# One slot of a software pipeline in another order: two-bank score tiles, the V products in one visit, a transpose over four quadrants

## The chip, the cores and the metric

The kernel runs on one core of one Trainium2 chip, as one launch. The metric is the device time of that launch in microseconds (us). A core has TensorE (PE, matrix products into PSUM), VectorE (DVE), ScalarE (ACT), GpSimd (POOL) and SyncE (SP); each works through its own queue in order, and they meet at semaphores. PSUM, the accumulator memory, has eight banks of 2 KiB per partition, and in this kernel all eight are in use, so that who holds which bank is part of the schedule.

## The reference

Attention with one added to the softmax's denominator, then a soft mixture of experts with slots, on the attention's output:

```
q, k, v: (8, 12, 448, 64)              # batch, heads, tokens, head size
scores = q @ k.T / 8
m = max(scores, -1);  e = exp(scores - m)
attn = e / (sum(e, -1) + exp(-m) + 1e-9)
x = (attn @ v), heads side by side      # (3584, 768)
logits = x @ phi                        # 32 slots
d = softmax(logits, over tokens);  slot_input = d.T @ x       # 8 experts of 4 slots
slot_out[e] = relu(slot_input[e] @ w1[e]) @ w2[e]             # 768 -> 1024 -> 768
c = softmax(logits, over slots);  out = c @ slot_out
```

## The kernel before, in words

The 96 heads are worked in 48 **pairs** n. A pair has its two heads on partitions 0 to 63 and 64 to 127; 448 tokens are three chunks of 128 (i = 0, 1, 2) and one of 64 (i = 3). For each pair these steps run, each written as a Python function that issues its instructions in order on several engines:

- `T(n)`: 28 transposes of 64x64 on PE (L256) into one PSUM bank of `psB`, then one copy of 128x896 to SBUF, on ACT (L263) or, for 4 pairs of 6 after the first nine, on DVE (L265).
- `A(n, i)`: the scores with queries on partitions, into a bank of `psA` (L285; L304 for i = 3, both heads in one bank), and their row maximum on DVE (L287, L307). `As` takes the next such step from the list `runs`, which is some three to four pairs ahead of the rest. A bank of `psA` is held from the product until the maximum has read it, and the pool has three, given out in turn.
- `W1`, `W2`, `W3`: once for three pairs, the maxima are negated on POOL, turned on PE and copied on ACT.
- `Bk(n, i)`: the scores with keys on partitions, both heads, into two banks of `psB`, minus the maximum by a second product (L367 and L370, or L396 and L399), and an exponential for each bank on ACT (L372, L402). With `mix` the two products of an `A` step are woven in between: `a0` first, `a1` last.
- `AV(n, i, qs)`: products of the exponentials with V (L436), 24 for the full chunks and 8 for the half one in every pair, into the one bank of `psV`.
- `N1`: copy of that bank to SBUF on ACT (L449). `N2`: sum and reciprocal on DVE (L464, L465), then the scaling on POOL (L469 to L480).
- `PX`: four products that turn the result (L501) into a bank of `psB`, and a copy on ACT (L507).

`P(b)` is the slot logits and their softmax for a batch of six pairs; its pieces are put into the slots by the table `post`. All of it is in an order written by hand (no scheduler moves anything). A string `ramp` orders the first three pairs. Then a loop over slots s runs, in two halves y = 0 and y = 1 for each slot: `Bk` i = 0 and 1 with two `A` steps, `AV` of the pair before (12 full products and the 8 half ones), `N1`; then `Bk` i = 2 with an `A` step, `Bk` i = 3 with the `A` step for i = 3, `T(s + 6)`, the first 12 `AV` products of pair s, `PX`, `N2`. POOL also issues the loads of q, k, v and the expert weights (L114, L176, L180, L181). After the loop the expert products and the output run (L853 and after).

The PSUM pools before are `psA` 3 banks, `psB` 4 and `psV` 1.

## Time and profile before

Three runs took 298.0, 298.18 and 299.7 us (median 298.18). The profiled execution has a span of 299.0 us from its first to its last instruction; no other time is recorded for that execution.

| stretch of the span, us | what runs | PE busy | DVE busy | ACT busy | POOL busy |
|---|---|---|---|---|---|
| 0 to 32 | ramp | 26.7 | 27.0 | 21.3 | 22.8 |
| 32 to 235 | slots with `A` steps | 198.8 | 190.7 | 193.6 | 164.6 |
| 235 to 250 | last slots, no `A` steps left | 14.7 | 8.3 | 13.6 | 6.4 |
| 250 to 299 | experts and output | 31.3 | 23.8 | 21.3 | 2.2 |

The table is added up from a view that gives each engine's busy time in stretches of the span. "Busy" of PE is modelled: matmuls are pipelined, and each is counted with its latency, so that 98% busy doesn't say that PE had no time left. DVE and ACT instructions overlap by some 0.1 us with the next one, so their cost in a row of instructions is the distance from start to start, not the duration of one.

### The profile page before, as it was taken

How to read it: one execution, taken by the hardware profiler on the slowest of the kernel's cores; microseconds unless marked ns; L12 is line 12 of the kernel's file. 1: busy time of each engine (PE TensorE's matmuls, PEld its weight loads, DVE VectorE, ACT ScalarE, POOL GpSimd, SP SyncE). 2: the span in 40 equal slices, each digit the busy share in tenths (PEclk: the TensorE clock that was granted, in tenths of full speed). 3: DMA queues.
4: the chain of work that ended last, by engine and by line, in shares of the span. 5: the costliest groups of instructions: out<-in, count | busy, mean ns of one | idle time of the engine just before them, and what ended most of it. 6: DMA issues, size and time to landing. Idle time of an engine off the chain costs nothing.

```text
span 299.0 us, 12398 instructions
## 1 busy us (share of the span) xinstructions
PE 271.4 (91%) x5174; PEld 162.5 (54%) x5174; DVE 249.7 (84%) x581; ACT 249.8 (84%) x559; POOL 195.9 (66%) x391
## 2 busy tenths in 40 slices
PE   5999899999999999999899999999999999996820
PEld 4445456566666566566556666656665555652100
DVE  5899799999999989999889999998999675537930
ACT  3569999999899989998989899989999987337820
POOL 8792887979696979887879697978686633000000
PEclk9999999999999999999999999999999999997555
DMA  7999998999999999999999999999799989908997
GB/s 132 147 143 208 149 138 138 188 165 188 185 204 179 184 176 202 163 182 182 202 159 184 176 199 152 196 183 196 125 150 187 213 185 263 344 10 318 380 453 322
DMA packets 47015, 58.67 MB, mean 196 GB/s; under 512 B 2800, under 2 KB 39920, under 8 KB 46704
## 3 DMA queue, kind: packets, MB, share of 16 engines
q0 software_dynamic: 40304, 42.29, 89.6%
q1 hardware_dynamic: 6656, 15.60, 13.8%
q8 instruction: 40, 0.66, 0.8%
q14 instruction: 15, 0.12, 0.1%
HBM read 89.16 MB, written 15.14 MB: 349 GB/s over the span
## 4 chain that ended last, share of the span: by engine, by line
PE 68%; ACT 10%; DVE 6%; POOL 6%; issue 4%; DMA 2%; DVEq 0%; POOLq 0%; ACTq 0%
PE ps_av L436 15%; PE ps_a L285 10%; PE ps_b L367 7%; PE ps_b L370 7%; PE ps_t L256 5%; PE ps_b L396 5%; PE ps_x L501 3%; PE ps_b L399 3%; ACT W L402 2%; PE ps_o L925 2%; DVE mx L298 2%; PE ps_s L623 2%; PE ps_h L862 2%; PE ps_so L882 2%; ACT W L263 2%
## 5 line engine op out<-in xcount | busy, mean ns | idle before, releaser
L287 DVE TENSOR_REDUCE mx<-ps_a 128x1 f32<-128x448 f32 x250 | 137.3, 613 | 4.6 <-PE ps_a L285 3.5
L372 ACT ACTIVATE W<-ps_b 128x448 bf16<-128x448 f32 x250 | 120.4, 574 | 0.0
L285 PE MATMUL ps_a<-W 64*128 64x448 bf16 x250 | 80.9, 352 | 0.0
L367 PE MATMUL ps_b<-W 64*128 64x448 bf16 x250 | 70.5, 352 | 1.1
L436 PE MATMUL ps_av<-W 128*128 128x65 bf16 (+1 forms) x1536 | 64.9, 196 | 2.2 <-issue 1.6
L436 PEld LDWEIGHTS <-W 128*128 128x128 bf16 (+1 forms) x1536 | 50.5, 100 | 30.2 <-issue 26.4
L370 PE MATMUL ps_b<-mT,sel 64*128 64x448 bf16 x250 | 66.5, 350 | 0.0
L469 POOL TENSOR_TENSOR W<-ubuf,rec 128x384 bf16<-128x384 f32 x44 | 36.3, 824 | 35.7 <-ACT W L507 19.3
L402 ACT ACTIVATE W<-ps_b 128x448 bf16<-128x448 f32 x86 | 46.1, 574 | 2.0 <-PE ps_b L399 2.0
L256 PEld LDWEIGHTS <-W 64*64 64x64 bf16 x1344 | 29.3, 112 | 12.7 <-issue 4.3
L507 ACT CAST W<-ps_x 128x512 bf16<-128x512 f32 x47 | 28.6, 608 | 7.4 <-PE ps_x L501 7.2
L256 PE MATMUL ps_t<-ident,W 64*64 64x64 bf16 x1330 | 30.6, 195 | 2.4 <-ACT W L215 1.4
L307 DVE TENSOR_REDUCE mx<-ps_a 128x1 f32<-128x448 f32 x48 | 29.5, 615 | 1.4 <-PE ps_a L304 1.4
L285 PEld LDWEIGHTS <-W 64*128 64x128 bf16 x250 | 23.4, 94 | 9.8
L114 POOL DMA_DIRECT2D W<-in_moe_w_dram x30 | 22.6, 755 | 7.9 <-PE ps_b L399 7.8
L370 PEld LDWEIGHTS <-sel 64*128 64x128 bf16 x250 | 19.6, 94 | 14.4 <-issue 5.6
L396 PE MATMUL ps_b<-W 64*64 64x448 bf16 (+1 forms) x134 | 27.1, 374 | 0.3
L449 ACT COPY ubuf<-ps_av 128x455 f32<-128x455 f32 x44 | 25.1, 571 | 0.8 <-POOL W L408 0.6
L399 PE MATMUL ps_b<-mT,sel 64*64 64x448 bf16 (+1 forms) x134 | 25.1, 354 | 0.1
L263 ACT COPY W<-ps_t 128x896 bf16<-128x896 bf16 x21 | 19.5, 927 | 6.5 <-PE ps_t L256 6.5
L298 DVE TENSOR_REDUCE mx<-ps_a 128x1 f32<-128x448 f32 x38 | 21.1, 616 | 1.9 <-PE ps_a L294 1.9
L480 POOL TENSOR_TENSOR W<-ubuf,rec 128x128 bf16<-128x128 f32 x44 | 17.5, 398 | 3.7
(156 smaller groups left out, 446.6 us busy)
## 6 DMA issues: line engine op xcount, KB each, us to landing
W<-in_moe_w_dram POOLq DMA_DIRECT2D x24, 768.0 KB, 9.9
W<-in_v_dram POOLq DMA_DIRECT2D x32, 192.0 KB, 6.5
out_dram<-W SPq DMA_DIRECT2D x2, 2688.0 KB, 10.0
W<-in_q_dram POOLq DMA_DIRECT2D x15, 336.0 KB, 6.3
W<-in_k_dram POOLq DMA_DIRECT2D x15, 336.0 KB, 7.5
stage<-in_moe_w_dram POOLq DMA_DIRECT2D x4, 768.0 KB, 9.6
W<-stage SPq DMA_DIRECT2D x4, 576.0 KB, 7.3
out_dram<-W SPq DMA_DIRECT2D x6, 384.0 KB, 3.0
```

What stands on the lines that cost most here:

```text
L256: nc.tensor.transpose(o, src[r, pl, tok * D:(tok + 1) * D], ident[r, r])
L285: nc.tensor.matmul(ps[:, 0:S], t[r, 0, i * 128:(i + 1) * 128], t[r, 1, :], start=True, stop=True)
L287: nc.vector.reduce_max(m[:, c:c + 1], ps[:, 0:S], axis=AX.X)
L307: nc.vector.reduce_max(mx[g][:, c:c + 1], ps[:, 0:S], axis=AX.X)
L367: nc.tensor.matmul(pss[hl][:, 0:S], t[rs[hl], 1, cols], t[rs[hl], 0, :], start=True, stop=False)
L370: nc.tensor.matmul(pss[hl][:, 0:S], sel[rs[hl], 2 * pl + hl:2 * pl + hl + 1].to_broadcast([64, 128]), mT[mg(n)][rs[hl], :], start=False, s ...
L372: nc.scalar.activation(e[:, hl, :], pss[hl][:, 0:S], AF.Exp, scale=scale)
L396: nc.tensor.matmul(outs[hl], t[rs[hl], 1, cols], t[rs[hl], 0, :], start=True, stop=False)
L399: nc.tensor.matmul(outs[hl], sel[rs[hl], 2 * pl + hl:2 * pl + hl + 1].to_broadcast([64, m]), mT[mg(n)][rs[hl], :], start=False, stop=True)
L402: nc.scalar.activation(e, p[:, 0:S], AF.Exp, scale=scale)
L436: nc.tensor.matmul(o, eT[n, i, hl][:, qc], vp[g % 2][:, 2 * pl + hl, i, 0:W65], start=(i == 0 and u == 0 and hl == 0) or (u == 3 and i == ...
L469: eng.tensor_mul(x[:, 0:3, c:c + 128].rearrange("p i (h d) -> p i h d", h=2), u[:, 0:6, 0:D].rearrange("p (i h) d -> p i h d", h=2), rec[: ...
```

## The change

The slot is written anew, and with it what it needs:

- `T` puts q of one head and k of the other into the same bank, so that its 28 transposes go in turn over four 64x64 quadrants. It now takes **two banks of `psA`**, and two copies of 128x448 read them: the first on ACT always, the second on DVE (on ACT for pairs 1 to 8). k is loaded with its two heads swapped, by two DMAs in place of one.
- `psB` becomes two tiles of two banks each. `X(n, i)` takes one such tile for both heads and runs one exponential of 128x896. `H(n)` (the half chunk) takes one too, and `PX` uses its second bank.
- `AV` runs the 8 half products, then `PX`, then the 24 full ones in one visit, for the pair before.
- `W2` takes a bank of `psA`; the buffer `wm` is there once in place of twice, `e1` twice in place of once.
- The order in a slot is `X` 0, `X` 1, `W1`, `T`, `H` with the `A` step for i = 3, `AV` half, `PX`, `AV` full, `N1`, `W2` and `W3`, `X` 2, `N2`. Each `X` has one `A` step woven in.

The diff, cut to its core:

```diff
-    sizes = [("nq0", 2 * NP * S), ("nq1", 2 * NP * S), ("nv", NATV), ("qk6", 2 * S), ("wm1", 512),
+    sizes = [("nq0", 2 * NP * S), ("nq1", 2 * NP * S), ("nv", NATV), ("qk6", 2 * S),
              ("qk0", 2 * S), ("qk1", 2 * S), ("qk2", 2 * S), ("wm0", 512), ("xTa", 4 * 512), ("qk3", 2 * S),
-             ("vp0", VPN), ("x0", 4 * DD), ("qk4", 2 * S), ("qk5", 2 * S), ("e2", NE * 2 * S), ("e1", S),
+             ("vp0", VPN), ("x0", 4 * DD), ("qk4", 2 * S), ("qk5", 2 * S), ("e2", NE * 2 * S), ("e1", 2 * S),
...
-        psB = pool("psB", 4, space=PSUM)
         psV = pool("psV", 1, space=PSUM)
-        pb_ = lambda nm: psB.tile([128, 512], F32, tag="b", name=nm)
+        psB = ExitStack()
+        banks = {"b": psB.enter_context(tc.tile_pool(name="psB", bufs=2, space=PSUM))}
+        two = lambda nm: banks["b"].tile([128, 2, 512], F32, tag="b", name=nm)
+        pb_ = lambda nm: banks["c"].tile([128, 512], F32, tag="c", name=nm)
...
-                gdma(out=t[:, l0:l1, :], in_=x[:, l0:l1, :])
+                if nm == "q":
+                    gdma(out=t[:, l0:l1, :], in_=x[:, l0:l1, :])
+                else:
+                    for r in range(2):
+                        gdma(out=t[rs[r], l0:l1, :], in_=x[rs[1 - r], l0:l1, :])
...
+        qcol = lambda tok: (2 * tok if tok < 4 else 2 * tok - 7) * 64
+
         def T(n):
             g, pl = divmod(n, NP)
-            first = n < NP * NP
-            ps = psB.tile([128, 2, S], BF16, tag="b", name="ps_t")
-
-            k0 = [psB.tile([128, 2, S], BF16, tag="b", name="ps_k") for _ in range(2)] if n == 0 else None
-            for a in range(2):
-                src = nat["qk"[a], g]
-                order = [(tok, hl) for tok in range(7) for hl in range(2)]
-                if a and n == 0:
-                    order.sort(key=lambda z: kcol(z[1], z[0]))
-                for tok, hl in order:
-                    c = kcol(hl, tok) if a else (2 * tok if tok < 4 else 2 * tok - 7) * 64
-                    r = slice(64 * hl, 64 * hl + 64)
-                    o = k0[c // 256][r, 0, c:c + 64] if a and n == 0 else ps[r, a, c:c + 64]
-                    nc.tensor.transpose(o, src[r, pl, tok * D:(tok + 1) * D], ident[r, r])
+            pss = [psA.tile([128, 1024], BF16, tag="a", name="ps_t") for _ in range(2)]
+            for tok in range(7):
+                for r in range(2):
+                    for z in range(2):
+                        nm, c = ("q", qcol(tok)) if z == r else ("k", kcol(z, tok))
+                        nc.tensor.transpose(pss[r][rs[z], c:c + 64], nat[nm, g][rs[r], pl, tok * D:(tok + 1) * D],
+                                            ident[rs[r], rs[r]])
             t = qk_t[n % NQK]
-            if n == 0:
-                nc.scalar.copy(t[:, 0, :], ps[:, 0, :])
-                nc.vector.tensor_copy(t[:, 1, 0:256], k0[0][:, 0, 0:256])
-                nc.vector.tensor_copy(t[:, 1, 256:S], k0[1][:, 0, 256:S])
-            elif first or n % 6 in (1, 3):
-                nc.scalar.copy(t, ps)
-            else:
-                nc.vector.tensor_copy(t, ps)
+            nc.scalar.copy(t[:, 0, :], pss[0][:, 0:S])
+            (nc.scalar.copy if 0 < n < NP * NP else nc.vector.tensor_copy)(t[:, 1, :], pss[1][:, 0:S])
...
-            ps = pb_("ps_m")
+            w = wm
+            ps = psA.tile([128, 512], F32, tag="a", name="ps_m")
...
+        def X(n, i, mix=False):
 
             g, pl = group[n]
             t = qkT[n]
+            cols = slice(i * 128, (i + 1) * 128)
+            e = e2_t[st["e2"] % NE]
+            st["e2"] += 1
+            ps = two("ps_b")
+
+            def score(hl):
+                nc.tensor.matmul(ps[:, hl, 0:S], t[rs[hl], 1 - hl, cols], t[rs[hl], hl, :], start=True, stop=False)
+
+            def bias(hl):
+                nc.tensor.matmul(ps[:, hl, 0:S], sel[rs[hl], 2 * pl + hl:2 * pl + hl + 1].to_broadcast([64, 128]),
+                                 mT[g][rs[hl], :], start=False, stop=True)
+
+            if mix:
                 a0, a1 = A(*runs.pop(0), steps=True)
                 a0()
                 score(1)
                 score(0)
                 bias(1)
                 bias(0)
+            else:
+                for f in (score, bias):
+                    for hl in range(2):
+                        f(hl)
+            nc.scalar.activation(e, ps[:, :, 0:S], AF.Exp, scale=scale)
+            if mix:
                 a1()
             for hl in range(2):
+                eT[n, i, hl] = e[:, hl, :]
+
+        def H(n, c=0):
+
+            g, pl = group[n]
+            t = qkT[n]
+            ps = halfs_[n] = two("ps_h")
+            for hl in range(2):
+                nc.tensor.matmul(ps[rs[hl], 0, 0:S], t[rs[hl], 1 - hl, 384:448], t[rs[hl], hl, :], start=True, stop=False)
             As(c)
             for hl in range(2):
+                nc.tensor.matmul(ps[rs[hl], 0, 0:S], sel[rs[hl], 2 * pl + hl:2 * pl + hl + 1].to_broadcast([64, 64]),
+                                 mT[g][rs[hl], :], start=False, stop=True)
+            e = e1_t[st["e1"] % 2]
+            st["e1"] += 1
+            nc.scalar.activation(e, ps[:, 0, 0:S], AF.Exp, scale=scale)
             for hl in range(2):
+                eT[n, 3, hl] = e
...
+        def AV(n, *steps):
+            end = n == NPAIR - 1
+            for half, chunks in steps or ((True, range(4)), (False, range(4))):
+                if n not in av:
+                    av[n] = av_tile(n)
+                    if end:
+                        av_half["ps"] = psA.tile([128, 512], F32, tag="a", name="ps_av")
+                a = av[n]
+                for i in chunks:
+                    for u in ([3] if half else range(3)):
+                        for hl in range(2):
+                            if half:
+                                t, z = (av_half["ps"], 0) if end else (a, 6 * W65)
+                                o, qc = t[rs[1 - hl], z:z + W65], slice(384, 448)
+                            else:
+                                c0 = (2 * u + hl) * W65
+                                o, qc = a[:, c0:c0 + W65], slice(u * 128, (u + 1) * 128)
+                            nc.tensor.matmul(o, eT[n, i, hl][:, qc], vp[g % 2][:, 2 * pl + hl, i, 0:W65],
+                                             start=i == 0 and (half or (end and u == 0 and hl == 0)),
+                                             stop=(i == 2 if end else i == 3), skip_group_check=True)
...
-        def PX(n):
+        def PX(n, ps):
             b, pb = divmod(n, PB)
             x, c = xb[b % 2], slice(pb * 128, pb * 128 + 128)
-            two = n == NPAIR - 1
-            pss = [pb_("ps_x") for _ in range(1 + two)]
+            last = n == NPAIR - 1
+            pss = [ps[:, 0, :], ps[:, 1, :]] if last else [ps[:, 1, :]]
...
-        runs = [(n, i) for n in range(NPAIR) for i in (0, 3, 1, 2)]
+        runs = [(n, i) for n in range(NPAIR) for i in (3, 0, 1, 2)]
...
-        rows_at = {77: 3, 83: 7, 85: 12, 89: 17, 91: 20, 92: 24, 93: 26, 95: 27}
+        rows_at = {77: 3, 83: 7, 85: 11, 89: 17, 91: 20, 92: 24, 93: 25, 95: 26}
...
+        ramp = ("T0 A A T1 A A W0 T2 A G0 A Y0 J0 A X0.0 A X0.1 A A T3 A X0.2 A A T4 H0.1 W1 A A Y1 T5 V0 "
+                "A X1.0 A K0 X1.1 A N0 X1.2 A T6 H1.1 A X2.0 M0 K1 A T7 X2.1 A V1 W2 T8 A "
+                "N1 X2.2 Q2 Y2 H2.1 Z0 M1 K2")
...
-        for s in range(3, NPAIR + 1):
-            for y in range(2):
-                hs = 2 * s + y
-                mix = len(runs) > 1 and runs[0][1] == 1 - y
-                if mix:
-                    Bk(s, 2 * y, mix=True)
-                    Bk(s, 2 * y + 1, y, mix=True)
-                else:
-                    As(1)
-                if mix:
-                    pass
-                elif s < NPAIR:
-                    Bk(s, 2 * y)
-                    side = int(y == 1 and len(runs) > 0 and runs[0][1] == 3)
-                    Bk(s, 2 * y + 1, side)
-                    As(1 - side)
-                else:
-                    As(1)
-                if y == 0:
-                    for i in (2, 3):
-                        AV(s - 1, i, range(3))
-                else:
-                    if s < NPAIR - 6:
-                        T(s + 6)
-                    if s and s + 1 in firsts:
-                        W2(mg(s + 1))
-                        W3(mg(s + 1))
-                    if s < NPAIR:
-                        for i in (0, 1):
-                            AV(s, i, range(3))
-                for f in post.get(hs, ()):
-                    f()
-                if y and 0 <= s - 2 < NPAIR - 2:
-                    PX(s - 2)
-                if y == 0:
-                    if 0 <= s - 1:
-                        for i in range(4):
-                            AV(s - 1, i, [3])
-                        if s == NPAIR:
-                            PX(s - 2)
-                        N1(s - 1)
-                        if not on_pool(s - 1):
-                            N2(s - 1)
-                else:
-                    if 0 <= s - 1 and on_pool(s - 1):
-                        N2(s - 1)
-                if y == 0 and s and s + 1 in firsts:
-                    W1(mg(s + 1))
...
+        for s in range(3, NPAIR):
+            mix = len(runs) > 1
+            X(s, 0, mix)
+            X(s, 1, mix)
+            if s + 1 in firsts:
+                W1(mg(s + 1))
+            if s < NPAIR - 6:
+                T(s + 6)
+            H(s, int(mix))
+            for f in post.get(2 * s, ()):
+                f()
+            late_loads(s)
+            AV(s - 1, (True, range(4)))
+            PX(s - 2, halfs_.pop(s))
+            AV(s - 1, (False, range(4)))
+            N1(s - 1)
+            for f in post.get(2 * s + 1, ()):
+                f()
+            if s + 1 in firsts:
+                W2(mg(s + 1))
+                W3(mg(s + 1))
+            X(s, 2, len(runs) > 0)
+            N2(s - 1)
+            end_loads(s)
+        n = NPAIR - 1
+        AV(n, (True, (0, 1, 3)), (False, (0, 1, 3)), (False, (2,)), (True, (2,)))
+        PX(n - 1, two("ps_x"))
+        N1(n)
+        N2(n)
```

163 lines of the change are left out of this document (54 added, 109 removed).

## The prediction

> **What bounds the kernel now.** I read the busy shares first, in slices of a fortieth of the span.
>
> ```profile
> span 299.0 us, 12398 instructions
> ...
> PE   5999899999999999999899999999999999996820
> ...
> DVE  5899799999999989999889999998999675537930
> ACT  3569999999899989998989899989999987337820
> ```
>
> Three engines are full from slice 3 to 31, so the shares don't tell which of them sets the pace. The order of instructions does. The timeline of DVE over one slot:
>
> ```profile
> 189.75 0.16 DVE L464 SCALAR_TENSOR_TENSOR rec<-ubuf,ec 128x7 f32<-128x7 f32 x1
> 189.94 0.20 DVE L465 RECIPROCAL rec<-rec 128x7 f32<-128x7 f32 x1
> 190.06 3.24 DVE L287 TENSOR_REDUCE mx<-ps_a 128x1 f32<-128x448 f32 x6
> 193.22 0.62 DVE L307 TENSOR_REDUCE mx<-ps_a 128x1 f32<-128x448 f32 x1
> 193.75 0.62 DVE L265 COPY W<-ps_t 128x896 bf16<-128x896 bf16 x1
> 194.28 0.16 DVE L464 SCALAR_TENSOR_TENSOR rec<-ubuf,ec 128x7 f32<-128x7 f32 x1
> ```
>
> DVE doesn't pause. From start to start, six maxima take 193.22 - 190.06 = 3.16, that is 0.53 each; the seventh 0.53; the copy of T 0.53; sum and reciprocal 0.31 (189.75 to 190.06). Sum 4.53, and the next slot's first maximum starts at 194.59, 4.53 after this one's. So DVE is the pace, as long as PE hands it products in time. How narrowly PE does that stands in PE's timeline of the same slot:
>
> ```profile
> 190.69 0.35 PE L285 MATMUL ps_a<-W 64*128 64x448 bf16 x1
> 190.97 0.79 PE L436 MATMUL ps_av<-W 128*128 128x65 bf16 x20
> 191.68 0.36 PE L285 MATMUL ps_a<-W 64*128 64x448 bf16 x1
> ...
> 192.36 0.38 PE L304 MATMUL ps_a<-W 64*64 64x448 bf16 x2
> ...
> 192.76 0.60 PE L256 MATMUL ps_t<-ident,W 64*64 64x64 bf16 x28
> ...
> 193.50 0.53 PE L436 MATMUL ps_av<-W 128*128 128x65 bf16 x12
> 193.87 0.39 PE L501 MATMUL ps_x<-ident,W 128*128 128x128 bf16 x4
> 194.18 0.36 PE L285 MATMUL ps_a<-W 64*128 64x448 bf16 x1
> ```
>
> Twice in a slot PE turns away from the scores: from the L285 at 190.69 to that at 191.68, and from the L304 at 192.36 to the L285 at 194.18. A product needs 0.36 and 0.04 until DVE starts on it. After the second break that is 194.18 + 0.40 = 194.58; DVE came free for it at 194.59. Such a break is bridged by products that lie finished in the three banks of `psA`: when the L304 starts, DVE still has that maximum and the two before it to do (0.53 each), the copy of T (0.53) and the sums (0.31). Where a batch's logits (24 products, 0.59) lengthen the first break, DVE runs dry at once:
>
> ```profile
> 114.91 2.22 DVE L287 TENSOR_REDUCE mx<-ps_a 128x1 f32<-128x448 f32 x4 [0.23 <-PE ps_a L285]
> 117.56 0.29 DVE L562 TENSOR_REDUCE cm<-ps_l 128x4 f32<-128x128 f32 x1 [0.44 <-ACT lb L558]
> 117.88 1.16 DVE L287 TENSOR_REDUCE mx<-ps_a 128x1 f32<-128x448 f32 x2
> ```
>
> 0.44 idle for 0.59 more of PE. So the reserve is some 0.1 us.
>
> **The parts of the change.**
>
> *T's copy.* DVE copied 896 columns at 0.53 in 4 slots of 6; now 448 in each. A 128-column copy (L628) holds DVE for 0.13 (189.62 to 189.75). The line through the two gives 0.30 for 448. DVE's mean goes from 0.35 to 0.30: 0.05 less a slot. ACT copied 896 columns at 0.80 (184.41 to 185.20) in 2 slots of 6, mean 0.27, and now does 448 in each, about the 0.45 of an exponential of that size: 0.18 more.
>
> *Exponentials.* Four of 448 stand 1.85 end to end, the last 0.57, so 0.43 each from start to start. One of 896 is not in the trace. Nearest is the 896-column ACT copy, 0.80; two singles make 0.86. I take 0.82, so three save 0.12 a slot. ACT's sum is about as before, and below the slot that follows.
>
> *PE.* T holds PE for 0.54 (192.76 to the ps_m product at 193.29); with four quadrants between half of that and the same. Changes of tile shape fall from six to four a slot, about 0.09 each (the L285 of 190.69 streams until 190.88 by the 0.19 between such products, the next kind starts at 190.97). That is 0.2 to 0.45 of PE, which doesn't set the pace.
>
> *The DMAs.* k's load is two instructions on POOL instead of one, 0.75 each for three slots (L176). POOL has 24.4 busy of 30, so it hides that; without cover it would be 0.25 a slot.
>
> *The banks.* This is the term that counts. T's two banks now come from the three of `psA`. Banks go round, so each taker waits for the third one before it. In a slot they are: X0 two products, X1 two, T two, H's L304, X2 two. So **H's product waits for the maximum of X1's second product**, and when it runs DVE has nothing in store but T's copy and that one product. After it PE does all of V's products, PX and the change of shape before X2's product. I call u the start of X1's second maximum and follow the chain:
>
> - its end: 0.61; to H's product: 0.04;
> - H's product and the two biases, to the next kind of work: 0.40 (192.36 to 192.76); change of shape 0.09;
> - 32 V products: 0.71 for 20 (190.97 to 191.68) and 0.37 for 12 (193.50 to 193.87), 1.08; PX 0.31 (193.87 to 194.18);
> - X2's product to DVE: 0.40. Sum 2.93.
> - Then DVE: X2's two maxima 1.06, sums 0.31 (N2 stands behind X2 in the queue), the next slot's X0 two and X1 first 1.59. Sum 2.96, and X1's second maximum is due.
>
> The cycle is 5.89 us against 4.53: **+1.36** for each slot. DVE has 0.53 + 0.30 + 0.53 to do in the 2.93 and is idle for the rest. T itself lies beside this: it waits for X1's first maximum (ends at u + 0.08) and with 0.54 ends at u + 0.67, when H's product may start at u + 0.65.
>
> The batch's pieces (logits 0.59, sums 0.69, small ones) stay, all in that gap. Before, six slots took 29.64 from one batch sum to the next (80.33 to 109.97 on DVE) where six plain ones are 27.2, so 2.4; after, PE's part of them is 0.59 + 0.69, five single products and two W2 (0.2 each), some 2.2. I count no difference. T is called in the loop for s = 3 to 41: 39 slots, 39 x 1.36 = 53.
>
> *Ramp.* DVE is dense there too (maxima back to back from 12 to 30 us). Eight T's after the first take two of three banks until ACT has copied both. Each can cost nothing, or T's 0.54 and a copy's 0.45. I take 0.5 for each, 4. *Last slots.* Three with A steps but no T have two more maxima in store; about 0.2 to 0.4 each, 1 in all. Slots without A steps stay within 1, and experts and output are as before.
>
> **Sum:** 53 + 4 + 1 = 58 on the span of 299.0, so 357. The median of the runs shown is 0.8 below the span: **356 us**.
>
> Bounds: if the 32 V products ran at the 0.025 of the batch sums (28 in 0.69) they would take 0.79, 0.29 less, and PX without its change of shape 0.1 less: +0.97 a slot, 38, ramp 0: 336. If T's end adds 0.15 and a batch's pieces 0.1 a slot, +1.61, 63, with 8 for the ramp: 371.
>
> **The rivals.**
>
> *PE is the bound.* For: 98% busy, and most of the chain that ended last lies on it. Against: DVE has no gap, and PE's maxima products wait on banks. If so, the change gives back T's half (0.27) and two changes of shape (0.18), 0.45 x 39 = 17.6: 281. The gain for T rests on four tiles running at once. The Trainium skill, "TensorEngine Tiling (Array Packing)", section "Key Properties", says that different tiles can load and multiply in parallel, which would give the 0.27; "TensorE: Matmul & The Clock Gate", section "Wait — 56ns, not 53.3ns?", says that start-to-start never falls below about 25 ns, which would leave T nothing to gain (then 0.18 x 39 = 7, so 291). This trace has 28 in 0.54, 19 ns each, already below that floor, so the measurement decides that the floor isn't one here, and leaves the gain open. Chance 5%.
>
> *DVE stays fed.* The break from H to X2 would have to be no longer than what DVE has in store, 0.83, against the 2.28 of the rows above; it decides as soon as a fourth bank or another order lets X1's maxima be waiting when H's product runs. Then only 0.05 x 39 = 2 is gained: 296. Chance 6%.
>
> *It does starve, by less.* PE's block streams better in one visit than any row shows, or H waits for an earlier bank: half of the 1.36, 27 us and 2 for the ramp: 327. Chance 12%.
>
> *The score tiles close a second loop.* Only two stand where four banks were, so X1's first score waits for X2's exponential. X2's bias ends some 0.75 after its first product started, that is 0.35 after its first maximum began; ACT adds 0.9, X1's products 0.6 and 0.4: X1's second product is ready at about 2.3, and DVE asks for it at 2.96. That leaves 0.6. If ACT is later by 1.1, behind N1's copy or a batch's exponentials, each slot loses 0.5 more: 375. Chance 9%.
>
> *T's four quadrants don't run at once.* T stays at 0.54 or grows by 0.3; the chain passes beside it, so 356 to 366, inside the forecast.
>
> **How the numbers follow.** The forecast has 68%. 336 to 371 holds most of that; with the starved-by-less and second-loop cases inside, the range is **322 to 375**. Three runs here lie within 0.6%, so 1% is about what can be told from no change. Faster by more than 1%: the 5% and part of the fed case, 8%. Within 1%: 4%. Slower: 88%.
>
> **What would show it.** In DVE's timeline after: one gap of over 1 us in each slot, between the maximum of H's product and the first of X2, released by PE's score product; plain slots of 5.9; DVE's busy share down to some 70%; T's copies of 0.4 on both engines. The working is wrong if DVE still runs without gaps, if the gap sits in another place (before X1: the score tiles; before T's copy: T), or if H's product starts before X1's second maximum has ended.

## The result, and the profile after

The changed kernel takes **375.2 us** (median of four runs, 374.8 to 375.9) against 298.9 us (four runs, 298.0 to 299.7): ratio 1.256, 95% interval 1.252 to 1.260. The forecast was 356 us with a range of 322 to 375, so the direction and most of the size came out, and the time lies just above the range, by 0.2 us. The profiled execution after, by the same parts of the page:

```profile
span 373.4 us, 12304 instructions
...
PE   3978887888788888988788888888887887899640
...
DVE  4776768687868787787768676867787763554850
ACT  3446878787878786878778877888787886634740
```

None of the three engines is full any more: DVE has 256.2 us of work, 69% of the span, where it was dense before. The timeline of DVE over one slot shows the hole (columns: start, duration, engine, line, what; in brackets how long the engine was idle before and what ended that):

```profile
203.04 1.68 DVE L284 TENSOR_REDUCE mx<-ps_a 128x1 f32<-128x448 f32 x3
204.72 0.39 DVE L262 COPY W<-ps_t 128x448 bf16<-128x448 bf16 x1
205.18 0.63 DVE L304 TENSOR_REDUCE mx<-ps_a 128x1 f32<-128x448 f32 x1
207.02 0.23 DVE L624 COPY cT<-ps_ct 128x128 bf16<-128x128 bf16 x1 [1.21 <-PE ps_ct L623]
207.31 1.16 DVE L284 TENSOR_REDUCE mx<-ps_a 128x1 f32<-128x448 f32 x2
```

X1's second maximum is the last of the three in the first line, so it starts at 204.10. The next maximum of a whole chunk, X2's first, starts at 207.31, 3.21 later; between them stand T's copy, H's maximum, a small copy of the batch and nothing else. PE over the same time:

```profile
203.71 0.22 PE L258 MATMUL ps_t<-ident,W 64*64 64x64 bf16 x2 [0.19 <-DVE mx L284]
204.24 0.41 PE L258 MATMUL ps_t<-ident,W 64*64 64x64 bf16 x26 [0.31 <-DVE mx L284]
...
204.77 0.38 PE L301 MATMUL ps_a<-W 64*64 64x448 bf16 x2
...
205.08 0.32 PE L432 MATMUL ps_av<-W 128*64 128x65 bf16 x8
205.82 0.38 PE L497 MATMUL ps_h<-ident,W 128*128 128x128 bf16 x4 [0.42 <-ACT W L395]
206.04 0.89 PE L432 MATMUL ps_av<-W 128*128 128x65 bf16 x24
...
206.92 0.36 PE L282 MATMUL ps_a<-W 64*128 64x448 bf16 x1
```

T waits twice for a maximum to set a bank free; H's product (L301) starts at 204.77, 0.05 after X1's second maximum has ended; then come V's half, PX, which waits 0.42 us for H's exponential, V's 24 products, and X2's product at last. The view of waits, summed over the span (columns: us in total, how many, longest):

```profile
DVE mx L284 <- PE ps_a L282: 32.7, 29, 1.6
...
PE ps_t L258 <- DVE mx L284: 19.3, 77, 0.3
...
PE ps_h L497 <- ACT W L395: 14.0, 37, 0.5
```

**Where the 74.4 us of span came from.** Four landmarks stand in both traces: the start of the slot loop's first `A`-step maximum (33.7, after 44.4), the start of slot 42 (39 slots with T later: 224.2, after 291.4), the start of slot 44 (233.0, after 302.2), and the first expert product on PE (256.7, after 330.5).

| stretch | forecast | measured |
|---|---|---|
| ramp | +4 | +10.7 |
| 39 slots with T (4.885 us each before, 6.333 after) | +53 | +56.5 |
| slots 42 and 43, `A` steps but no T | +1 | +2.1 |
| slot 44 to the experts | within 1 | +4.6 |
| experts and output | 0 | +0.6 |

The profiled execution of the kernel before is a long one: its other spans on record are 295.8 to 298.8. One of its slots takes 7.67 (143.4 to 151.1), where the slots at the same place of the other batches take 5.9 to 6.1; PE stands still in it for 1.10 ahead of 150.01, for no cause that the profile shows. So differences to its loop, here and below, are some 1.7 us too small; by the times of the runs the change costs 76.3.

### The profile page after: what moved, and what is told of

Same layout as the page of the kernel before. It is cut to its first block, busy times and chain, and to the rows that moved or that the text cites. A ratio compares the mean times of both kernels' runs of the same rounds, so it can differ in the third digit from the quotient of the medians.

```text
span 373.4 us, 12304 instructions
## 1 busy us (share of the span) xinstructions
PE 296.6 (79%) x5174; PEld 169.9 (46%) x5174; DVE 256.2 (69%) x592; ACT 264.0 (71%) x449; POOL 205.6 (55%) x409
## 4 chain that ended last, share of the span: by engine, by line
PE 41%; DVE 35%; ACT 16%; issue 3%; DMA 1%; DVEq 0%; SPq 0%; ACTq 0%
DVE mx L284 27%; PE ps_av L432 10%; PE ps_t L258 6%; ACT W L395 6%; ACT W L261 5%; PE ps_h L497 5%; PE ps_a L282 4%; DVE mx L295 3%; ACT W L376 2%; DVE rec L461 2%; PE ps_o L904 2%; PE ps_l L531 2%; PE ps_s L619 2%; PE ps_h L841 1%; PE ps_b L359 1%
## 5 line engine op out<-in xcount | busy, mean ns | idle before, releaser
L284 DVE TENSOR_REDUCE mx<-ps_a 128x1 f32<-128x448 f32 x250 | 138.5, 610 | 33.1 <-PE ps_a L282 32.7
L376 ACT ACTIVATE W<-ps_b 128x896 bf16<-128x896 f32 x144 | 122.8, 917 | 17.6 <-PE ps_a L282 8.3
L432 PE MATMUL ps_av<-W 128*128 128x65 bf16 (+1 forms) x1536 | 58.8, 196 | 0.2 <-ACT W L376 0.2
L258 PE MATMUL ps_t<-ident,W 64*64 64x64 bf16 x1344 | 30.8, 200 | 26.4 <-DVE mx L284 19.3
L258 PEld LDWEIGHTS <-W 64*64 64x64 bf16 x1344 | 24.6, 111 | 55.3 <-issue 51.1
L261 ACT COPY W<-ps_t 128x448 bf16<-128x448 bf16 x48 | 25.5, 532 | 28.4 <-PE ps_t L258 28.4
L503 ACT CAST W<-ps_h 128x512 bf16<-128x512 f32 x45 | 26.4, 586 | 18.0 <-PE ps_h L497 17.8
L359 PEld LDWEIGHTS <-W 64*128 64x128 bf16 x288 | 20.6, 94 | 35.5 <-issue 28.8
L282 PEld LDWEIGHTS <-W 64*128 64x128 bf16 x250 | 23.2, 93 | 16.5 <-issue 6.0
L497 PE MATMUL ps_h<-ident,W 128*128 128x128 bf16 x180 | 17.4, 218 | 14.0 <-ACT W L395 14.0
L395 ACT ACTIVATE W<-ps_h 128x448 bf16<-128x448 f32 x48 | 26.1, 544 | 1.6 <-PE ps_h L391 0.7
L362 PEld LDWEIGHTS <-sel 64*128 64x128 bf16 x288 | 23.0, 95 | 8.7 <-issue 1.0
L184 POOL DMA_DIRECT2D W<-in_k_dram x34 | 21.1, 629 | 0.0
## 6 DMA issues: line engine op xcount, KB each, us to landing
out_dram<-W SPq DMA_DIRECT2D x2, 2688.0 KB, 10.7
```

Source lines behind the costliest of these rows:

```text
L258: nc.tensor.transpose(pss[r][rs[z], c:c + 64], nat[nm, g][rs[r], pl, tok * D:(tok + 1) * D], ident[rs[r], rs[r]])
L261: nc.scalar.copy(t[:, 0, :], pss[0][:, 0:S])
L282: nc.tensor.matmul(ps[:, 0:S], t[r, hl, i * 128:(i + 1) * 128], t[r, 1 - hl, :], start=True, stop=True)
L284: nc.vector.reduce_max(m[:, c:c + 1], ps[:, 0:S], axis=AX.X)
L359: nc.tensor.matmul(ps[:, hl, 0:S], t[rs[hl], 1 - hl, cols], t[rs[hl], hl, :], start=True, stop=False)
L362: nc.tensor.matmul(ps[:, hl, 0:S], sel[rs[hl], 2 * pl + hl:2 * pl + hl + 1].to_broadcast([64, 128]), mT[g][rs[hl], :], start=False, stop=True)
```

## The experiments

Each kernel ran beside the kernel before, on the same chip (297.6 to 299.0 us there), once each, `e6_before_t4` four times. This table cuts each span at three landmarks that all of them have on DVE: the start of the second reciprocal of `N2` ("ramp"), from there to the start of the 43rd ("loop", 41 pairs), and from there to the DVE instruction that opens the experts (it writes `band`; "tail"). What is left behind it is 40.4 to 41.3 in all, but 42.4 in `e11_no_t`. A time is 1.8 above the span of the same execution; the expectations and the text name now one, now the other. The times of before, after and `e6_before_t4` are medians, so that before and `e6` show another distance.

| kernel | time | span | ramp | loop | tail |
|---|---|---|---|---|---|
| before | 298.9 | 299.0 | 33.5 | 199.4 | 25.7 |
| after | 375.2 | 373.4 | 44.3 | 257.9 | 30.3 |
| e1_t_one_bank | 359.7 | 357.9 | 39.5 | 247.7 | 30.3 |
| e2_t_psB | 355.2 | 353.4 | 39.5 | 242.8 | 30.3 |
| e3_px_late | 361.3 | 359.5 | 44.3 | 244.4 | 30.0 |
| e4_split_v | 392.5 | 390.7 | 44.8 | 275.0 | 29.6 |
| e5_t_last | 356.7 | 354.9 | 45.0 | 238.8 | 30.3 |
| e6_before_t4 | 305.6 | 304.7 | 36.3 | 201.6 | 25.7 |
| e7_before_v1 | 313.8 | 311.9 | 34.9 | 209.5 | 27.0 |
| e8_order | 345.6 | 343.8 | 43.4 | 229.5 | 30.0 |
| e9_tail | 378.8 | 377.0 | 44.9 | 257.9 | 33.1 |
| e10_all | 340.5 | 338.7 | 37.9 | 229.1 | 30.8 |
| e11_no_t | 338.1 | 336.3 | 44.3 | 219.3 | 30.3 |
| e12_before_exp | 311.8 | 310.0 | 36.9 | 204.6 | 27.6 |
| e13_before_exp_t | 334.2 | 332.4 | 35.0 | 229.0 | 27.6 |
| e14_tail_h | 373.8 | 372.0 | 44.4 | 257.9 | 28.8 |
| e15_all_old_order | 336.7 | 334.9 | 43.8 | 220.9 | 29.4 |
| e16_exp_v1 | 325.7 | 324.0 | 36.5 | 215.8 | 30.4 |

### First set, on the kernel after: T's banks, PX, V's visit

`e1_t_one_bank`: T and k's load as before, its one bank from `psA`.

```diff
-            pss = [psA.tile([128, 1024], BF16, tag="a", name="ps_t") for _ in range(2)]
+            pss = [psA.tile([128, 2, S], BF16, tag="a", name="ps_t") for _ in range(2 if n == 0 else 1)]
```

> The changed kernel, with T and k's load as before (two quadrants, q and k of both heads in one bank, one copy of 896 columns), that bank taken from psA. T so takes one of the three banks, not two. Theory (psA's banks set the slot): H's product waits for X1's first maximum, one earlier; it starts about 0.5 sooner in slots whose copy is on DVE, and 0.1 sooner where ACT copies 896 columns ahead of H's exponential. Plain slots 5.6 and 6.0 against 6.09, the whole 14 us less in the loop and some us less in the ramp: about 355. Rival (the single visit of V makes the gap, banks don't matter): slots of 6.1 or, by T's longer time on PE, 6.3; 373 to 382.

Span 357.9. Plain slots with T's copy on DVE take 5.67, with it on ACT 6.04, as expected. The loop is 10.2 shorter, 0.25 us a slot, where 14 was expected. T's two quadrants and its longer copies are in that figure too, so it isn't the price of the bank alone.

`e2_t_psB`: T over four quadrants, its two banks from a score tile.

```diff
-            pss = [psA.tile([128, 1024], BF16, tag="a", name="ps_t") for _ in range(2)]
+            t2 = banks["b"].tile([128, 2, 1024], BF16, tag="b", name="ps_t")
+            pss = [t2[:, 0, :], t2[:, 1, :]]
```

> The changed kernel, with T's two banks taken as one two-bank tile of psB in place of two banks of psA; nothing else. Theory (psA's banks set the slot): H's product needs X0's second maximum only; it is then held by H's score tile, free when X1's exponential ends, about 0.6 sooner than now. Slots of about 5.5, 23 us less in the loop, some 4 in the ramp: about 346. Rival (banks of psA don't matter): 373. Rival (the two score tiles are the tighter loop, five takers in place of four): slower than 373.

Span 353.4 where 346 was expected, plain slots 5.6 to 5.7 where 5.5 was: with `psA` whole, H's score waits 0.31 for X1's exponential instead, as the score tile's next user. 15 us of the loop and 4.8 of the ramp come back.

`e3_px_late`: PX behind V's 24 products.

```diff
-            PX(s - 2, halfs_.pop(s))
             AV(s - 1, (False, range(4)))
+            PX(s - 2, halfs_.pop(s))
```

> The changed kernel, with PX's four products behind the 24 full products of V in place of ahead of them. In the changed kernel they wait 0.42 to 0.49 for the exponential of H, which reads the other bank of the same tile. Theory (PE's way from H's product to X2's sets the slot): the wait is covered by V's products, X2 comes 0.37 sooner, slots 5.7 against 6.09, 39 x 0.37 = 14 less: 359. Rival (DVE or ACT would take up what PE gains, or the wait only moves): 371 to 374.

Span 359.5, as expected, and plain slots of 5.62 in place of 6.09. So PX's wait for H's exponential, which the prediction hadn't foreseen, is on the path: PX writes the second bank of the tile whose first bank that exponential reads, and it waits though the banks are different ones.

`e4_split_v`: V's products in two visits, chunks 0 and 1 where they were, 2 and 3 behind X2, and `N2` after the next slot's X0.

```diff
+            if 3 < s <= NPAIR - 4:
+                N2(s - 2)
...
-            AV(s - 1, (False, range(4)))
-            N1(s - 1)
+            split = s < NPAIR - 4
+            AV(s - 1, (False, (0, 1) if split else range(4)))
+            if not split:
+                N1(s - 1)
...
-            N2(s - 1)
+            if split:
+                AV(s - 1, (False, (2, 3)))
+                N1(s - 1)
+            else:
+                N2(s - 1)
```

> The changed kernel, with V's full products in two visits: chunks 0 and 1 ahead of X2, chunks 2 and 3 behind it (up to pair 42), and the sums of N2 one half slot later, behind the next slot's first X, since the copy N1 ends later. Theory (the visit's length counts in full, since DVE has nothing in store): the way to X2 is shorter by 12 products, 0.41; slots 5.7, 39 x 0.41 = 16 less: 357. Rival (the time comes back between X2 and the next X, or N1's later copy holds the sums): 365 to 375.

Span 390.7 where 357 was expected, a miss. Two things come together. With `N2` put off, POOL's scaling comes later, and PE's weight load for PX now waits for POOL, 20.1 us in all (no weight load of PX waits for POOL in the kernel after). And TensorE's clock was granted at a half in this run, for 3.4 us at a time (once 6.8), in ten slots of the loop and in no slot of the kernel after. In the row of the page each digit is the clock in a fortieth of the span, in tenths; first the kernel after, then `e4_split_v`:

```profile
PEclk9967999999999999999999999999999999999755
PEclk9958889899999899998989896999898999999755
```

The ten are just the slots of 8.0 and more. Slots at the same places of a batch, at the full clock, take 6.7, so the clock makes about 15 of the loop's 17 us more. Without it the loop would be at some 260, no shorter than the 257.9 of the kernel after: plain slots of 5.81 are outweighed by those of 6.7. The edit moved two things, so it doesn't answer what V's visit costs in this order; in the order of before, `e7` and `e16` do.

### Second set: T behind V; two parts alone

`e5_t_last`: H and its `A` step ahead of the V products as before, T moved from in front of H to right ahead of X2.

> The changed kernel, with T moved behind V's products, right ahead of X2 (and W2), so that H's product comes before T's banks in the round of psA. T keeps its two banks of psA. Theory: H's product then needs X0's second maximum only and starts about 1.0 sooner; two more products lie in store when PE turns to V. PX waits for H's exponential, X2 comes about 0.8 sooner in the slot: slots of 5.3, 39 x 0.8 = 32 less: 341. Rival (T's mere holding of two of three banks is what costs, wherever it stands): X2's products wait for T's copies, slots of 6 or more, 370 to 380.

Span 354.9 where 341 was expected: plain slots 5.43 against 5.3 expected, but slots with a batch's logits or `W2` stay at 6 to 6.7. H's product starts 0.39 before X1's second maximum does, so the place of T ahead of H is what tied H to that maximum. PX still waits 0.42.

`e6_before_t4` and `e7_before_v1` put one part of the change alone on the kernel before: T over four quadrants with two of `psB`'s four banks (and k's load in two), or V's full products in one visit:

```diff
-                    for i in (2, 3):
+                    for i in range(0 if s > 3 else 2, 4):
                         AV(s - 1, i, range(3))
...
-                    if s < NPAIR:
-                        for i in (0, 1):
-                            AV(s, i, range(3))
```

> The kernel before with one part of the change alone: T over four quadrants in two banks, with its two copies of 448 and k's heads swapped, the banks from psB (four banks there). Theory: DVE sets the slot before, T's copy falls from 0.35 to 0.30 a slot on average and PE's second break gets shorter by 0.3, which lets DVE run through where a batch's sums lengthen it: 2 to 6 us less in the loop, 2 more in the start (k's first load in two pieces): 293 to 298. Rival (ACT, with 0.16 more a slot, becomes the bound): 303 to 306.

A time of 305.6 us, ratio 1.022 (1.017 to 1.027), where 293 to 298 was expected; it lies where the rival put it, 303 to 306. TensorE's time for T shrinks (26 transposes from 163.42 to 163.76, a change of shape within, where 28 took 0.54), and nothing comes back; 2.3 of the 5.7 us of span are the start (first maximum at 8.12 instead of 5.83). ACT, which the rival names, has 144.6 busy of 150 us (60 to 210), where it had 142.0. And T, with two banks of the score pool in place of one, waits there for an exponential, 3.9 us in 11 waits. Which of the two costs the rest isn't settled. The Trainium skill, "TensorEngine Tiling (Array Packing)", section "PSUM Bottleneck", says that packing tiles speeds up TensorE and not the reading of PSUM, which may then be the bottleneck. This run agrees with it: PE is quicker, and the time is not.

> The kernel before with one part of the change alone: V's 24 full products in one visit, in the first break of the slot, 12 products more there and 12 fewer in the second. Theory (a break longer than what psA's three banks hold costs DVE the excess): the first break is 0.41 longer with a reserve of 0.1, so each slot loses 0.3: 41 x 0.3 = 12 more, 311. Rival (the visit costs in full, as with no store): 0.41 x 41 = 17 more, 316. Rival (one visit saves changes of shape, and DVE catches up): 298.

A time of 313.8, between the 311 expected and the rival's 316: +10.1 in the loop, 0.25 us a pair (some 12 with the kernel before's one long slot set right, as expected), 1.4 in the ramp and 1.3 in the tail.

### Third set: the order, the tail, all together, and no T

`e8_order`: H, V's half, V's 24, PX, T, `W2`, X2.

```diff
-            if s < NPAIR - 6:
-                T(s + 6)
             H(s, int(mix))
...
-            PX(s - 2, halfs_.pop(s))
             AV(s - 1, (False, range(4)))
+            PX(s - 2, halfs_.pop(s))
...
+            if s < NPAIR - 6:
+                T(s + 6)
             if s + 1 in firsts:
```

> Order of a slot: A step, X1, H, V's half, 24 full V products, PX, T, W2, X2. H's product comes at the start of X1's second maximum minus about 0.4 us (as in the run with T behind H), PX comes when H's exponential is long over, and between H's product and X2's stand the V products (1.08 us), PX (0.31) and T with its shape changes (0.4). Theory that the scores of X2 and H behind the V visit and behind the wait of PX set the slot, and T's banks only where they are taken early: plain slots about 5.0 us, the loop 39 x 1.1 = 43 us shorter, span about 330 to 335. Rival, that T's two banks cost the same wherever T stands (ahead of X2 its banks must come from the maxima of the step before): plain slots 5.4 or more, span 348 or more.

Span 343.8: the loop is 28 us shorter, not 43. Plain slots are 4.95 to 5.3 as expected; slots with a batch's logits or `W2` in the break are 5.8 to 6.6. DVE's timeline in two slots of it:

```profile
204.59 0.39 DVE L262 COPY W<-ps_t 128x448 bf16<-128x448 bf16 x1 [0.58 <-PE ps_t L258]
...
210.22 0.29 DVE L568 TENSOR_REDUCE sm<-ps_lT 128x1 bf16<-128x128 f32 x1 [0.83 <-PE ps_lT L566]
...
211.44 1.18 DVE L284 TENSOR_REDUCE mx<-ps_a 128x1 f32<-128x448 f32 x2 [0.44 <-PE ps_a L282]
```

With everything between H and X2 in one break, DVE runs dry there in a plain slot too (0.58, the first line), and a slot with a batch's piece has 0.83 and 0.44.

`e11_no_t` leaves T out of the slots (`qkT[s + 6] = qk_t[(s + 6) % NQK]` in its place), so that they work on q and k turned in the ramp.

> T(s+6) is left out of the slots (its 28 transposes, two banks and two copies): the slots read the q and k turned in the ramp, so the computation of these pairs is not the reference's. Theory that T costs the change its two banks' place ahead of H: plain slots about 5.0 instead of 6.1 us, loop 39 x 1.1 = 43 us shorter, span about 330. Rival, that only T's own work counts (DVE's half copy of 0.39 us and TensorE's 0.3 to 0.5): plain slots 5.5, span about 350. Third, that the V visit and PX alone set the slot: 6.0, span 370.

Span 336.3, plain slots 5.03. So T's presence, with its banks, transposes and copies, costs 38.6 of the loop's 58.5, about 1 us a slot, though PE's and DVE's time for it is only some 0.25 and 0.31. The other 20 are there without T.

`e9_tail`: the last four slots with X2 behind V's half, PX and the six full products of V's chunk 0, and the other 18 behind X2 (the expectation counts eight and 24).

> Only the last four slots differ from the kernel after: X2's scores stand behind V's half and the first chunk's eight products instead of behind all 32, the other 24 behind X2. Theory that the single visit of V is what makes the last slots longer (no A step is left as store): the stretch from slot 44 to the experts gives back 3 to 4 of its 4.6 us, span about 370. Rival, that it is the two-bank score tile's one exponential that X1 and X2 wait for (0.65 to 0.69 us a slot): the stretch stays within 1 us of the 28.3 us that it has, span 372.5 to 374. The slots before are as they were in both.

Span 377.0: the tail grows by 2.8, where it was to shrink by 3 to 4, or stay within 1. ACT in the kernel after has a hole ahead of X2's exponential in both of the last two slots:

```profile
318.19 2.54 ACT L376 ACTIVATE W<-ps_b 128x896 bf16<-128x896 f32 x3 [1.05 <-PE ps_b L362]
320.62 0.54 ACT L395 ACTIVATE W<-ps_h 128x448 bf16<-128x448 f32 x1
321.63 0.59 ACT L503 CAST W<-ps_h 128x512 bf16<-128x512 f32 x1 [0.47 <-PE ps_h L497]
323.27 0.92 ACT L376 ACTIVATE W<-ps_b 128x896 bf16<-128x896 f32 x1 [1.05 <-PE ps_b L362]
```

In `e9_tail`, at the same place, X2's exponential comes without a hole, and one stands ahead of the next slot's X0:

```profile
319.53 0.92 ACT L376 ACTIVATE W<-ps_b 128x896 bf16<-128x896 f32 x1
321.03 1.73 ACT L376 ACTIVATE W<-ps_b 128x896 bf16<-128x896 f32 x2 [0.58 <-PE ps_b L362]
```

Splitting the visit moves ACT's wait. In the slots ahead of these, X2 and X0 both have one (0.67 and 1.09), where the kernel after has one of 1.47. The clock has a part in the 2.8 as well: it was granted at a half from 310.0 to 313.5 and from 330.5 to 333.9, and nowhere in the tail of the kernel after. The tail's last stretch, behind the last reciprocal, takes 8.47 for 7.37, so the second of these cost about 1.1. What the first cost isn't settled, so it stays open whether the split alone would have left the tail within 1.

`e10_all`: the order of `e8` in the loop, of `e9` in the last slots, T's banks of the ramp from a score tile, and half of k's first load on ACT's queue.

> The order of the first of these four kernels in the loop, the second's order in the last four slots, T's banks of the ramp from the score tiles' pool, and the second half of k's first load issued by ACT's queue. If the parts add up: the loop 43 us shorter, the tail 3 to 4, the ramp 5 (T's banks, as the run with T's banks from that pool had its ramp's end at 39.5 instead of 44.3) plus about 1.5 of the load: span 373.4 - 53 = about 320. Rival, that the loop's order gives only half of it (T's banks cost wherever T stands): about 342.

Span 338.7. The ramp gives back 6.3, as expected (5 + 1.5); the loop is that of `e8`, so 14 of the 43 us hoped for aren't there, and the tail gives nothing back. The whole lies 19 above the expectation and 3 below the rival.

### Fourth set: the third part alone, and the tail again

`e12_before_exp`: the kernel before with two-bank score tiles and one exponential; PX in H's tile, T's and `W2`'s one bank from `psA`. `e13_before_exp_t` has T's bank in a score tile instead.

```diff
-                pss = [pb_("ps_b") for _ in range(2)]
-                outs = [p[:, 0:S] for p in pss]
+                ps = two_("ps_b")
+                outs = [ps[:, hl, 0:S] for hl in range(2)]
...
-            for p, e in zip(pss, es):
-                nc.scalar.activation(e, p[:, 0:S], AF.Exp, scale=scale)
+            if i < 3:
+                nc.scalar.activation(e, ps[:, :, 0:S], AF.Exp, scale=scale)
```

> The kernel before with the third part alone: two score tiles of two banks with one exponential for X, H's second bank for PX, W2's and T's bank from the A steps' three; T itself, V's two visits and the order are as before. Theory that a bank of the three taken for T costs the slot its share of the store (the run of the changed kernel with T's two banks cut to one has slots 0.6 to 0.9 us longer than the one without T): slots 4.5 + 0.4 to 0.6, span 315 to 322. Rival, that two score tiles for four users a slot close a loop of their own with ACT and that this sets the slot: 5.2 or more, span 326 or more. Third, that nothing is late in this order: 298 to 301.

Span 310.0, some 5 below the expected range: +5.2 in the loop (0.13 a pair), 3.4 in the ramp, 1.9 in the tail. A bank of `psA` for T costs little in the order of before: no more than these 0.13, which the score tiles share.

> The run ahead of this one, but T's one bank is in a score tile, which then has five users a slot. Theory that the place of T's bank decides: the A steps keep their three banks, so about 298 to 304. Rival, that the two score tiles with five users set the slot (T waits for an exponential, and the next scores for T's copy): 315 or more.

Span 332.4, the rival. The view of waits names it:

```profile
PE ps_t L262 <- ACT W L384: 23.1, 39, 0.9
```

0.59 us in each of 39 slots: T waits for an exponential. The same bank, taken from the other pool, costs 24 us more in the loop.

`e14_tail_h`: the kernel after, but in the last three slots H's scores and PX have a bank of `psA` each.

```diff
-            ps = halfs_[n] = two("ps_h")
+            if n >= NPAIR - 3:
+                ps = psA.tile([128, 1, 512], F32, tag="a", name="ps_h")
+            else:
+                ps = halfs_[n] = two("ps_h")
```

> Only the last three slots differ from the kernel after: H's scores and PX go to banks of the A steps' pool, so that the two score tiles have only X as users. Theory that the tail is the loop of PE and ACT through the two score tiles (X1's and H's scores wait 0.65 and 0.25 us a slot, and ACT stands 1.05 to 1.47 us ahead of X's exponential): each of the three slots loses 0.5 to 0.9 us, span 371 to 372. Rival, that the V visit in front of X2 is what ACT stands for, wherever H has its bank: within 0.5 us of 373.4.

Span 372.0, and the tail is 1.5 us shorter (28.8), as the first theory had it. The wait of PX's copy is gone in two of the three slots:

```profile
319.86 0.54 ACT L398 ACTIVATE W<-ps_h 128x448 bf16<-128x448 f32 x1
320.35 0.58 ACT L507 CAST W<-ps_x 128x512 bf16<-128x512 f32 x1
321.99 0.92 ACT L376 ACTIVATE W<-ps_b 128x896 bf16<-128x896 f32 x1 [1.06 <-PE ps_b L362]
```

In the third, where a batch's sums stand ahead of PX, it is 0.47 for 0.78. PX no longer waits for H's exponential: in the first of the three it starts at 309.42, and that exponential only at 309.49. So it was the shared tile that made it wait. The hole ahead of X2 stays, 1.06.

### Fifth set: do the parts add up?

Alone, T over four quadrants costs 7.2 us, V's visit 15.3, the score tiles 13.6 (each against the kernel before on its chip), 36 in all; the change costs 76 by the same measure. `e15_all_old_order` has all three parts, and the order of instructions of the kernel before. `e16_exp_v1` has the score tiles and V's visit, and T as before.

> All three parts of the change on the kernel before, with its order of a slot kept: T over four quadrants with two banks of the A steps' three, two-bank score tiles with one exponential, V's 24 full products and 8 half ones in the first break, H and T behind X2, PX last. If the parts add up: 298.2 + 7.4 + 15.4 + 13.6 = 335, so that the change's order of a slot, with T, H and V in the same break, costs the other 40. Rival, that the parts cost one another their banks in any order: 365 to 380.

> Two of the parts on the kernel before, in its order: two-bank score tiles with one exponential (T's one bank from the A steps' three) and V's products in one visit in the first break; T as before. If they add up: 298.2 + 15.4 + 13.6 = 327. Rival, that two score tiles let PE come back from the longer visit too late: 340 or more.

Times of 336.7 and 325.7 us: they add up, within some 2 us. From the changed kernel `e15` differs in the order of the instructions (that of the ramp and of the `A` steps too) and in which two SBUF buffers are double. So **38.5 of the 76 us are the price of the order**, 37.0 of these in the loop. DVE over a slot of `e15_all_old_order`:

```profile
178.53 0.39 DVE L264 COPY W<-ps_t 128x448 bf16<-128x448 bf16 x1
...
179.40 2.22 DVE L286 TENSOR_REDUCE mx<-ps_a 128x1 f32<-128x448 f32 x4 [0.17 <-PE ps_a L284]
181.88 1.16 DVE L286 TENSOR_REDUCE mx<-ps_a 128x1 f32<-128x448 f32 x2 [0.26 <-PE ps_a L284]
```

Two holes of 0.17 and 0.26 in a slot stand where the kernel after has one of over 1 us. Two banks of `psA` for T in place of one (with its quadrants and k's load) cost 5.1 of the loop here (220.9 - 215.8), and 10.2 in the changed order (257.9 - 247.7, `e1`).

No version tried beats the kernel before.

## Why the prediction was right in the slot, and wrong around it

**The step that failed** is what the sum put outside the 39 slots with T: 4 for the ramp, 1 for the slots without T, nothing for the start, the last slots and the experts, 5 in all. Measured are 10.7, 2.1, 4.6 and 0.6, 18.0 in all. The ramp is the term most mis-sized, and the last slots one put at nothing. What each is made of stands below.

**What bounds the kernel now: right, though not all of it is shown.** DVE is the pace: the hole in its row stands where it was forecast, and it is PE's product that ends it. That PE's own time had no part isn't shown by `e6`, which shortens PE's T and gains nothing, since ACT's share and T's wait for a bank grow in it. One line was misread: the gap of 0.44 at 117.56, from which the reserve of 0.1 was taken, was ended by ACT's copy of the logits (L558), as the line says, and not by a product of the scores; the next of those starts at 117.41 and comes later still. The sum doesn't use the reserve.

**The banks: right in its links, short by 0.20.** Plain slots take 6.09 for the 5.89 forecast. The chain, link by link, in the slot shown above:

| link | forecast | measured |
|---|---|---|
| end of X1's second maximum, H's product starts | 0.65 | 0.67 |
| H's product and biases, change of shape | 0.49 | 0.31 |
| V's half, PX | 0.58 | 0.96, of which 0.42 PX's wait |
| V's 24 | 0.81 | 0.72 |
| a batch's single product | not in a plain slot | 0.16 |
| X2's product to DVE | 0.40 | 0.39 |
| then DVE, until X1's second maximum again | 2.96 | 2.93 |

The missing link is that PX shares H's tile. It took more than the better streaming of the rest gave back. A batch costs 38.19 - 6 x 6.09 = 1.65 beyond six plain slots, where I counted its 2.4 unchanged. So the plain slots' 0.20, 7.8 over 39, was for the most part made up by batches that came some 5 cheaper, and that 39 slots came to 56.5 for 53 is in part luck.

What the step didn't say is that **the place of T's banks in the order makes them dear**. Of the loop's 58.5 us, 19.1 come back when T moves behind V's products and keeps its banks (`e5`), 15.1 when its banks come from a score tile (`e2`), and 38.6 when T is gone with all its work (`e11`). The other 20 are there without T. I put them down to the length of the break: V, PX, `W2` and a batch's pieces between one `A` step and the next. The kernel before pays them in two breaks, and DVE's store is filled again between the two. That part is argued, not shown: V's visit alone costs 10 of the loop in the order of before (`e7`), and `e4`, which was to test it in the new order, doesn't.

**T's copy, Exponentials, PE: right, and off the path.** T's copy holds DVE for 0.31 (204.59 to 204.90 in `e8`; forecast 0.30). Three exponentials of 896 take 2.54, so 0.81 from start to start (forecast 0.82). T's last 26 transposes pass between 204.24 and 204.46: 0.22. That is the half of 0.54 (which had a change of shape in it) that I took as the best case.

**The DMAs: wrong at the start.** I looked at k's loads in the loop, where POOL hides them. k's first load is split in two as well, ahead of the first T, and nothing hides that one: the first maximum starts at 8.16 instead of 5.83, also in `e6` (8.12). It lies at 7.72 to 8.59 in every kernel with that load and at 5.78 to 6.29 in every one with the old; with the second half on ACT's queue it is 7.15. That is 2.3 us that are not in the sum.

**Ramp: the term that failed most, 4 against 10.7.** T's two banks were sized well: 5.0 (`e15` less `e16` is 7.3, of which 2.3 are the load; `e2` gives back 4.8) against 4. Left out were the load, and the two score tiles with V's visit: 3.0 (`e16` less before), with T and the load as they were. The same ramp ends anywhere from 43.4 to 45.0 in eight kernels here, so these parts hold within about 1.

**Last slots: wrong.** "Stay within 1" went by the missing `A` steps and thought of no second store. The score banks are one, for ACT, and the change makes it coarser: H's scores took one bank of four, now one tile of two. V's visit alone lengthens the tail by 1.3, the score tiles alone by 1.9, both by 3.7 in `e15`, with the order of before too. (`e16` has 4.7; its tail is that of `e15` up to the last stretch, which takes 8.35 for 7.35, with the clock granted at a half from 277.7 to 281.1.) So most of the 4.6 comes with the two parts, whatever the order. 1.5 of it is H's and PX's use of those tiles (`e14`); the rest isn't divided further, since the split of `e9` only moved the wait. The 0.6 in the experts wasn't looked into.

**The rivals.** "PE is the bound" named 281 to 291, and fell with the time itself. "DVE stays fed" fell, and its condition too: in `e5` X1's second maximum is still waiting when H's product runs, and the slot is 5.43, not 4.5, because the break is longer than any store in it. "Starves by less" would have needed better streaming. There was some, 0.31 a slot of the 0.68 that it takes (0.18, 0.04 and 0.09 in the table, PX's wait apart), and that wait outweighed it. "A second loop by the score tiles" named 375, and the time is 375, but not by its mechanism: it had X1's scores late, and those wait only in the last slots. The score tiles do close a wait on ACT in each slot, at PX. "T's quadrants don't run at once" fell.

The reason that the range missed is that the forecast's upper bound put 8 us on the ramp and nothing more on the tail or the start: the loop's 56.5 were well inside its 63, the 18 us outside the loop were not inside its 9. (Its sum, 299.0 + 63 + 8 + 1 - 0.8, is 370, not 371.) That the miss is as small as 0.2 us is luck: the range's end of 375 came from the rival of the score tiles, which didn't happen.

## What to carry to other kernels

Where one engine sets the pace and another feeds it through a few PSUM banks, the banks are the store that bridges each absence of the feeder. Ask of a new order how long each single absence is and what lies finished when it begins. A sum of busy time doesn't show this: three parts cost 36 us, and the order in which they were put 38 more. Look at the granted clock, too, before a cause is given for a slow stretch: in `e4_split_v` it was half the clock that made the slots of over 8 us. When an edit changes a resource's pool, go through all of its users (ramp, first load, last slots), not only the steady slot. Sharing a tile between two engines' users can make one wait for the other even where the banks differ.

## What the runs showed of the hardware

Transposes of 64x64 that go in turn over four quadrants run at 8.5 ns each: 26 in 0.22 us, from start to start on PE up to the next kind of product. Over two quadrants it was 28 in 0.54, a change of shape of 0.09 within, so 16 ns each. One by one, they start about 3 ns apart in fours, one to each quadrant, and a quadrant's next one starts some 31 ns after its last (in pairs, some 29 ns, over two quadrants). The Trainium skill, "TensorEngine Tiling (Array Packing)", section "Key Properties", says that different tiles can load and multiply in parallel; the trace agrees. The Trainium skill, "TensorE: Matmul & The Clock Gate", section "Wait — 56ns, not 53.3ns?", says that start-to-start never falls below about 25 ns; these 8.5 ns don't agree, so where instructions go to different tiles that isn't a floor. Within one quadrant the 31 and 29 ns stay above it.

The granted clock fell to a half in the ramp of the kernel after, and not in `e5_t_last`, whose ramp has the same order of work. In the view of stretches (the clock is the third number from the end), the kernel after:

```profile
24.00:27.00 3.00, 2.80 (x12) 0.76 (x11) 2.84 (x6) 0.68 (x2) 1.91 (x5) 0.50 1.16 193
```

and `e5_t_last`:

```profile
24.00:27.00 3.00, 2.81 (x10) 0.46 (x8) 2.15 (x4) 1.37 (x3) 2.11 (x6) 1.00 1.19 205
```

Yet the ramp ends at 44.3 in the first and at 45.0 in the second. Of the eight kernels with this ramp, five had half the clock in it for 6.8 to 10.3 us and end it at 43.4 to 44.8; three had the full clock and end it at 44.4 to 45.0. So it cost nothing that can be seen there. In the loop of `e4_split_v` it did: a slot with 3.4 us at half the clock took 8.0 to 8.2 where its likes at the full clock took 6.7, so 1.3 to 1.5 more. What lowers the clock was not tried.
